# The folded scans of an attention and Fourier kernel: 64 rows of each half of the array instead of 48

## The chip, the cores and the metric

The kernel runs on one core of a Trainium2 chip. The metric is the device time of one execution in microseconds (us), here the median of three runs; lower is better.

## The reference, cut to what matters

Inputs: `x` of 2048 rows and 512 columns, `wqkv` (512 x 1536), `wo` (512 x 512), four Fourier matrices and a gate vector.

```
g = sigmoid((x * gate_w).sum(-1))
q, k, v = x @ wqkv, cut into 32 heads of 16 columns
p = softmax(q k^T / 4)              # each head: 2048 x 2048
a = (p v) @ wo
b = dft_seq_re @ (x @ dft_hid_re.T) - dft_seq_im @ (x @ dft_hid_im.T)
out = g * a + (1 - g) * b
```

All is float32. The softmax needs a shift for every row that lies near the row's largest score; the kernel gets it from a pass of its own over the scores, the *scan*. The scan's result only sets this shift, which cancels in the quotient.

## The kernel before, in words

**Two halves of the array.** Nearly every product on TensorE takes 64 of its 128 rows or fewer. `halves_of` (L199 to L203) issues two products, one in rows 0 to 63 and one in rows 64 to 127, which run side by side. Such a pair is called a *step* below. A float32 operand is split into an upper part (hi) and the rest (lo), and a product is the sum of hi*hi, hi*lo and lo*hi, three steps.

**Stages.** The first stage projects `x` to q, k and v (`project_t`, `project_s`) and applies the Fourier matrix of the columns; the second applies the Fourier matrix of the rows (the loop over `coef`, L711 to L777, whose products are `xy<-b,c` in the profile). Then comes the attention: 16 pairs of heads, in which the scores (L228), the exponential (L252, L260) and the product with the values (L806) alternate.

**Scans.** A pair of heads has 64 scans: 16 blocks of 128 queries by 4 chunks of 512 keys. A scan makes one product for each of the two heads: head j in rows 64j and up, with 128 queries standing and 512 keys moving. `row_loads` (L104 to L115) fills the two tiles `qs` and `ks` for one pair of heads by eight DMAs: for each half, 32 rows hold hi of a key's 16 numbers twice over against hi and lo of the query's, and 16 rows more hold lo of the key against hi of the query. So a product takes 48 of the 64 rows of its half.

**Scans beside the other products.** Scans are put between the steps of the first two stages by `beside` (L326): one scan every so many steps, set by `scan_at` (BESIDE 2.72, SWAP 2.97, PART 2.15). The first 64 scans (pair 0) are plain: one DVE reduction takes the maximum of both heads (L155). The next 644 are *folded* (`scan_folded`, L159): for a pair of key chunks a and b, DRAM holds a - b and b (`kf_d`). The product with a - b goes through ACT's Relu into a tile `fold` (L176); the product with b goes to DVE, which adds `fold` and takes the maximum (L178). So of two scans in turn, one gives ACT two operations and the next gives DVE two. A scan's second head is issued one scan late, so a step L172 on PE holds head 0 of scan n and head 1 of scan n - 1. The PSUM banks of folded scans are `d0`, `d1`, `k0`, `k1` (and for some stretches a spare pair), taken in turn by `bed` (L290): a bank is written again two scans after it was last written, and PE waits there until ACT or DVE has read it.

**Loads of the folded scans.** `load_scan_beside` (L320) calls `row_loads` for pair 0 with plain keys and for the 11 other pairs of this phase with `kf_d`, and issues the eight DMAs on SP's queue seven steps apart, between the loads of the Fourier coefficients (`craw`, L395) and the stores (L316). `ROWS` says at which scan; a folded pair's loads begin some 24 to 60 scans ahead of its first scan.

The scans after the 708th (L153, beside the attention) are plain and have 48 rows; the scores of the attention (L228) have 50.

Of the kernel before, what the change touches and what calls it, by code (L numbers as in the profile page):

```python
# [18 lines left out]
P = 128  # L19
S = 2048  # L20
D = 512
H = 32
DH = 16
# [43 lines left out]
def build(tc, xT, wqkv, wo, wrT, wiT, cr, ci, ct, gate, out):  # L67
    nc = tc.nc
    with ExitStack() as ctx:
# [7 lines left out]
        q_d = [dram.tile([P, 2, S], F32, name=f"q_d{f}") for f in range(ND)]  # L77
        k_d = [dram.tile([P, 2, S], F32, name=f"k_d{f}") for f in range(ND)]
        ks_d = [dram.tile([P, S], F32, name=f"ks_d{f}") for f in range(ND)]
        kf_d = [dram.tile([P, 2, S], F32, name=f"kf_d{f}") for f in range(ND)]  # L80
# [20 lines left out]

        scanned, used, unfolded = {}, {}, {}

        def row_loads(p, queue, keys=k_d):  # L104

            qs = stk.tile([P, S], F32R, tag="stk", name="qs")
            ks = stk.tile([P, S], F32R, tag="stk", name="ks")
            loads = []
            for j in range(2):
                b, r = 64 * j, slice(DH * ((2 * p + j) % 8), DH * ((2 * p + j) % 8) + DH)  # L110
                loads += [(ks[b:b + 32, :], keys[p // 4][r, 0:1, :].to_broadcast([DH, 2, S])),
                          (qs[b:b + 32, :], q_d[p // 4][r, :, :].rearrange("e n s -> (e n) s")),
                          (ks[b + 32:b + 48, :], keys[p // 4][r, 1, :]),
                          (qs[b + 32:b + 48, :], q_d[p // 4][r, 0, :])]
            return (qs, ks), [lambda dst=dst, src=src: queue.dma_start(dst.bitcast(F32), src) for dst, src in loads]  # L115

        def load_scan(p):
            if p < NP:
                scanned[p], loads = row_loads(p, nc.sync)
                for load in loads:  # L120
                    load()

        def load_use(p, spread=False):
            if p < NP:
                used[p], loads = row_loads(p, nc.sync)
                for load in loads:
                    load()
                    if spread:
                        yield
                qs, ks = used[p]  # L130
                for j in range(2):
                    b = 64 * j + 48
                    nc.sync.dma_start(ks[b:b + 2, :].bitcast(F32), ones_d)
                    for n in range(2):
                        nc.sync.dma_start(qs[b + n:b + n + 1, :].bitcast(F32),
                                          m_d[p][n:n + 1, :, j].rearrange("n g b k -> n b g k"))
# [3 lines left out]
        def new_maxima(p):  # L140
            mx[p] = (sm.tile([P, 2, NB, 4], F32, tag="mx_end", name="mx", bufs=1) if p == END_PAIR else
                     sm.tile([P, 2, NB, 4], F32, tag="mx", name="mx"))
# [16 lines left out]
        def scan_folded(n, j, bank, pool):  # L159

            p, i = SEQ[n]
            qb, c = i // 4, i % 4
            if i == 0 and j == 0:
                new_maxima(p)
                if p in PARTS:
                    nc.vector.memset(mx[p], -3.0e38)
            qs, ks = scanned[p]  # L170
            b, ps = 64 * j, bank(n, j)
            nc.tensor.matmul(ps, qs[b:b + 48, qb * P:(qb + 1) * P], ks[b:b + 48, c * 512:(c + 1) * 512],  # L172
                             start=True, stop=True)
            if c % 2 == 0:
                fold[j] = pool.tile([P, 512], F32, tag=f"fold{j}", name="fold")
                nc.scalar.activation(fold[j], ps, AF.Relu)  # L176
            else:
                nc.vector.tensor_tensor_reduce(out=fold[j], in0=ps, in1=fold[j], scale=1.0, scalar=-3.0e38,  # L178
                                               op0=ALU.add, op1=ALU.max, accum_out=mx[p][:, j, qb, c // 2:c // 2 + 1])
# [56 lines left out]
        def bank():  # L236

            order_.append(order_.pop(0))
            return narrow(order_[-1], "s2")
# [29 lines left out]
        with ExitStack() as pf:  # L269
# [31 lines left out]
            def after(n, f, *args):  # L301

                count[0] += 1
                due.append((slots[0] + n, count[0], f, args))
# [11 lines left out]
                    d[2](*d[3])  # L316

            def load_scan_beside(p):
                scanned[p], loads = row_loads(p, nc.sync, kf_d if p else k_d)
                for n, load in enumerate(loads):  # L320
                    after(7 * n, load)

# [3 lines left out]
            def beside():  # L326

                slots[0] += 1
                run_due()
                if pace[0] is None:  # L330
                    return
                pace[1] += 1.0 / pace[0]
                while seen[0] < FRONT and pace[1] >= 1.0:
                    pace[1] -= 1.0
                    n = seen[0]
                    if n == FOLDED.start:
                        begin_folds()
                    if n in ROWS:
                        load_scan_beside(ROWS[n])
                    if n not in FOLDED:  # L340
                        scan(n, s1())
                        done = n
                    else:

                        scan_folded(n, 0, *beds)
                        done = behind(n - 1)
                    seen[0] += 1
                    if seen[0] == FRONT:
                        done = behind(n)
                    if done is not None and SEQ[done][1] == SCANS - 1:  # L350
                        for d, part in enumerate(shift(SEQ[done][0], nc.scalar.copy, nc.gpsimd.tensor_sub)):
                            maxima.append(part)
                            after((3, 8, 26, 31, 36)[d], part)
# [3 lines left out]
            def behind(n):  # L357
                if n in FOLDED:
                    scan_folded(n, 1, *beds)
                    return n  # L360
# [59 lines left out]
            with ExitStack() as px:  # L420
# [185 lines left out]
                for n, (w, dst, f, c) in enumerate(order):  # L606
                    lead = s1() if n in (0, 2, 4, 6) else None
                    project_t(w, dst, f, c, lead and (lead[:, 0, :], lead[:, 1, :]))
                    if n == 7:
                        gate_sums()  # L610
                after(22, load_scan_beside, 0)
                after(84, scan_at, PACE)
                for f, c in [(2, 0), (3, 0)] + [(f, c) for f in range(1, ND) for c in range(1, NC)]:
# [60 lines left out]
            with ExitStack() as py:  # L674
# [36 lines left out]
                for n, (ph, t, u) in enumerate(coef):  # L711
# [38 lines left out]
                    for w in range(CS):  # L750
                        s = u * CS + w
# [29 lines left out]
        with ExitStack() as pa:  # L781
# [443 lines left out]
            for step in range(NP * PERIODS):  # L1225
                p, i = step // PERIODS, step % PERIODS
# [133 lines left out]
```

## Time and profile before

| | |
|---|---|
| median of 3 runs | 1714.61 us (1714.26 to 1715.05) |
| the profiled execution | 1714.2 us, span 1712.4 us from first to last instruction |
| PE busy | 1701.0 us, 99% of the span |
| ACT, DVE, POOL busy | 1492.3, 1188.9, 765.4 us |
| chain that ended last | 97% PE |
| stretch of the folded scans | 133.7 to 653 us |
| granted TensorE clock | 0.999 of full speed |

The profile is of one execution. Its chain of work that ended last is followed back from the last instruction; 97% of it is TensorE. A line of a group gives the program line, engine, operation, the tile written and the tiles read, partitions x elements, the count, the busy time and the mean of one. PE stands for the products, PEld for the loads of the standing operand, which overlap them. Products run side by side and are pipelined, so their mean duration is longer than the time from one to the next.

### The profile page before, as it was taken

Reading aid. Unit: us, or ns where it says so; the run is one execution under the profiler, and the core shown is the slowest. Engines: PE = TensorE matmul, PEld = TensorE weight load, DVE = VectorE, ACT = ScalarE, POOL = GpSimd, SP = SyncE. Lnnn points to the kernel's source line nnn. Section 1 sums busy time; section 2 is a strip of 40 time slices with the busy share of each in tenths; the row PEclk is TensorE's granted clock in tenths of the full one; section 3 lists DMA queues with packets and bytes.
Section 4 is the critical chain, followed back from the end, with each engine's and each line's share of the span. In section 5 each row is a group of like instructions: output and inputs, shape, how many; then the busy total and the mean of one; then the engine's idle time right before and its main releaser. Section 6 shows DMA issues by size and latency. Waiting matters only on the chain.

```text
span 1712.4 us, 36306 instructions
## 1 busy us (share of the span) xinstructions
PE 1701.0 (99%) x13560; PEld 1022.5 (60%) x13560; DVE 1188.9 (69%) x2179; ACT 1492.3 (87%) x2472; POOL 765.4 (45%) x909
## 2 busy tenths in 40 slices
PE   9999999999999999999999999999999999999998
PEld 6888888989988885333333333333345555555554
DVE  5898888889899996666666666666742556654343
ACT  6447889888888888999999999999998888889876
POOL 3672435755555762433535455353423333334222
PEclk9999999999999999999999999999999999999999
DMA  7783457533337665356544445353436465566733
GB/s 255 244 288 77 149 161 217 160 111 108 105 105 206 175 133 101 94 132 141 137 112 113 121 117 132 100 130 79 98 71 145 133 150 148 141 171 156 195 90 127
DMA packets 148961, 240.96 MB, mean 141 GB/s; under 512 B 50048, under 2 KB 60784, under 8 KB 142192
## 3 DMA queue, kind: packets, MB, share of 16 engines
q1 hardware_dynamic: 133520, 217.27, 47.1%
q0 software_dynamic: 14688, 20.33, 5.1%
q8 instruction: 106, 1.74, 0.5%
q10 hardware_dynamic: 576, 1.05, 0.2%
q14 instruction: 71, 0.58, 0.1%
HBM read 158.34 MB, written 81.01 MB: 140 GB/s over the span
## 4 chain that ended last, share of the span: by engine, by line
PE 97%; DMA 1%; DVE 0%; issue 0%; ACT 0%; SPq 0%; DVEq 0%; ACTq 0%
PE pvb L806 29%; PE xy L203 26%; PE s L228 19%; PE s L172 9%; PE s L203 8%; PE s L153 5%; DMA q_d<-eh 0%; DMA raws<-wqkv 0%; DMA raws<-xT 0%; PE s L595 0%; DVE y L921 0%; DVE fold L178 0%; ACT fold L176 0%; SPq L565 0%; SPq L564 0%
## 5 line engine op out<-in xcount | busy, mean ns | idle before, releaser
L252 ACT ACTIVATE eb<-s 128x1024 f32<-128x1024 f32 x512 | 581.0, 1135 | 59.8 <-PE s L228 59.7
L260 ACT ACTIVATE e<-s 128x512 f32<-128x512 f32 x1022 | 611.0, 713 | 0.0
L155 DVE TENSOR_REDUCE mx<-s 128x2 f32<-128x1024 f32 x380 | 460.9, 1224 | 196.5 <-PE s L153 196.3
L806 PE MATMUL pvb<-eb,va 128*17 128x512 f32 x2052 | 514.5, 597 | 0.0
L806 PE MATMUL pvb<-e,va 128*17 128x512 f32 x2044 | 513.6, 597 | 0.0
L178 DVE CUSTOM_DVE_ANT_0 fold<-s,fold 128x512 f32<-128x512 f32 x644 | 433.2, 690 | 57.0 <-PE s L172 30.4
L176 ACT ACTIVATE fold<-s 128x512 f32<-128x512 f32 x644 | 377.4, 602 | 81.3 <-PE s L172 61.8
L228 PEld LDWEIGHTS s<-qs,ks 50*128 50x128 f32 x2048 | 214.3, 184 | 361.6 <-ACT eb L252 269.2
L228 PE MATMUL s<-qs,ks 50*128 50x512 f32 x2048 | 424.3, 435 | 0.0
L203 PE MATMUL xy<-b,c 64*128 64x512 f32 x2448 | 390.9, 393 | 0.3 <-ACT c L371 0.3
L172 PE MATMUL s<-ks,qs 48*128 48x512 f32 x1288 | 315.4, 402 | 1.5 <-DVE mx L178 0.9
L203 PEld LDWEIGHTS xy<-b,c 64*128 64x128 f32 x2448 | 284.0, 187 | 30.5 <-issue 1.0
L172 PEld LDWEIGHTS s<-ks,qs 48*128 48x128 f32 x1288 | 171.3, 184 | 36.1 <-DVE mx L178 9.9
L806 PEld LDWEIGHTS pvb<-eb,va 128*17 128x17 f32 x2052 | 69.8, 96 | 189.1 <-issue 179.5
L153 PE MATMUL s<-ks,qs 48*128 48x512 f32 x760 | 153.2, 394 | 0.0
L203 PE MATMUL s<-b,b 64*128 64x512 f32 x1050 | 136.8, 391 | 0.0
L825 POOL DMA_DIRECT2D r_d<-lc x31 | 18.0, 580 | 262.2 <-DVE lc L824 213.7
L203 PE MATMUL xy<-w,b 64*128 64x512 f32 x768 | 114.8, 392 | 0.0
L203 PEld LDWEIGHTS s<-b,b 64*128 64x128 f32 x1050 | 100.2, 185 | 23.7 <-issue 1.0
L818 POOL DMA_DIRECT2D lc<-ob x124 | 63.0, 515 | 114.6 <-DVE ob L815 109.3
L403 POOL TENSOR_TENSOR c<-craw,c 128x512 fp32r<-128x512 f32 x84 | 110.2, 1312 | 6.7
L827 POOL DMA_DIRECT2D rb<-r_d x124 | 60.5, 495 | 107.0 <-DMA r_d<-lc 101.8
(149 smaller groups left out, 1560.9 us busy)
## 6 DMA issues: line engine op xcount, KB each, us to landing
qs<-q_d SPq DMA_DIRECT2D x68, 256.0 KB
craw<-cr SPq DMA_DIRECT2D x60, 256.0 KB
craw<-ct SPq DMA_DIRECT2D x48, 256.0 KB
ks<-k_d SPq DMA_DIRECT2D x46, 256.0 KB
kept_None<-sum SPq DMA_DIRECT2D x40, 256.0 KB
craw<-kept_None SPq DMA_DIRECT2D x40, 256.0 KB
qs<-q_d SPq DMA_DIRECT2D x68, 128.0 KB
craw<-ci SPq DMA_DIRECT2D x32, 256.0 KB
```

The lines of the kernel that those rows point to most:

```text
L153: nc.tensor.matmul(ps[:, j, :], qs[b:b + 48, qb * P:(qb + 1) * P], ks[b:b + 48, c * 512:(c + 1) * 512], start=True, stop=True)
L155: nc.vector.tensor_reduce(mx[p][:, :, qb, c], ps, axis=AX.X, op=ALU.max)
L172: nc.tensor.matmul(ps, qs[b:b + 48, qb * P:(qb + 1) * P], ks[b:b + 48, c * 512:(c + 1) * 512], start=True, stop=True)
L176: nc.scalar.activation(fold[j], ps, AF.Relu)
L178: nc.vector.tensor_tensor_reduce(out=fold[j], in0=ps, in1=fold[j], scale=1.0, scalar=-3.0e38, op0=ALU.add, op1=ALU.max, accum_out=mx[p][:, ...
L203: nc.tensor.matmul(ps[j], lhs[r], rhs[r], start=first, stop=last)
L228: nc.tensor.matmul(pss[j], ks[b:b + 50, kb * P:(kb + 1) * P], qs[b:b + 50, q0:q0 + 512], start=True, stop=True)
L252: nc.scalar.activation(e, ps, AF.Exp, scale=SCALE)
L260: nc.scalar.activation(e[j], pss[j], AF.Exp, scale=SCALE)
L403: sub(lo, raw, hi.bitcast(F32))
L806: nc.tensor.matmul(pvb[r:r + VC, :], va[:, kb, 2 * p + j, :], es[c][j], start=kb == 0, stop=kb == NB - 1, tile_position=(0, r))
L818: nc.gpsimd.dma_start(lc[32 * n:32 * n + 32, :], ob[r + DH:r + VC, :].rearrange("p (s e) -> p s e", e=16))
```

## The change

`row_loads` gets an argument `square`, which `load_scan_beside` sets for every pair but pair 0. With it, the last two loads of each half have 32 rows instead of 16: lo of the key twice over against hi and lo of the query. So 16 rows more carry lo*lo. The products of `scan_folded` read 64 rows instead of 48. Pair 0's scans, the scans beside the attention and the scores keep their rows.

```
-        def row_loads(p, queue, keys=k_d):
+        def row_loads(p, queue, keys=k_d, square=False):
...
-                          (ks[b + 32:b + 48, :], keys[p // 4][r, 1, :]),
-                          (qs[b + 32:b + 48, :], q_d[p // 4][r, 0, :])]
+                          *([(ks[b + 32:b + 64, :], keys[p // 4][r, 1:2, :].to_broadcast([DH, 2, S])),
+                             (qs[b + 32:b + 64, :], q_d[p // 4][r, :, :].rearrange("e n s -> (e n) s"))] if square else
+                            [(ks[b + 32:b + 48, :], keys[p // 4][r, 1, :]),
+                             (qs[b + 32:b + 48, :], q_d[p // 4][r, 0, :])])]
...
-            nc.tensor.matmul(ps, qs[b:b + 48, qb * P:(qb + 1) * P], ks[b:b + 48, c * 512:(c + 1) * 512],
+            nc.tensor.matmul(ps, qs[b:b + 64, qb * P:(qb + 1) * P], ks[b:b + 64, c * 512:(c + 1) * 512],
...
-                scanned[p], loads = row_loads(p, nc.sync, kf_d if p else k_d)
+                scanned[p], loads = row_loads(p, nc.sync, kf_d if p else k_d, p > 0)
```

No instruction changes its place on any engine. On SP's queue, at the loads of the second folded pair in the first stage, before the change (lines of `row_loads`: L115; `ab_d` is a store of the other work; the last numbers are the rows and the row's elements):

```order
L115 DMA ks<-kf_d_87 32x1x2048
L115 DMA qs<-q_d_75 32x2048
L316 DMA ab_d_118<-ab 128x512
L115 DMA ks<-kf_d_87 16x2048
L115 DMA qs<-q_d_75 16x2048
```

and with it (lines are two further on):

```order
L117 DMA ks<-kf_d_87 32x1x2048
L117 DMA qs<-q_d_75 32x2048
L318 DMA ab_d_118<-ab 128x512
L117 DMA ks<-kf_d_87 32x1x2048
L117 DMA qs<-q_d_75 32x2048
```

The order stays; the second load of each tile is twice as large. On PE, in the second stage, two folded scans among the steps of the Fourier products (a row with x2 is a step; its shape is that of the result), before:

```order
L172 MATMUL s<-ks,qs 128x512 x2
L203 MATMUL xy<-b_4856,c 128x512 x2
L203 MATMUL xy<-b_4855,c 128x512 x2
L172 MATMUL s<-ks,qs 128x512 x2
L203 MATMUL xy<-b_4886,c 128x512 x2
```

and with the change:

```order
L174 MATMUL s<-ks,qs 128x512 x2
L205 MATMUL xy<-b_4856,c 128x512 x2
L205 MATMUL xy<-b_4855,c 128x512 x2
L174 MATMUL s<-ks,qs 128x512 x2
L205 MATMUL xy<-b_4886,c 128x512 x2
```

The rows are the same but for their line numbers: only the number of array rows that L172 reads differs, which a row of this list doesn't show.

## The prediction

> **What bounds the kernel now.** I read the page first (busy shares and the chain that ended last), then a table of stretches for PE, then the timeline of PE at three places, then the waits. The page says that TensorE is the bound nearly everywhere:
>
> ```profile
> PE 1701.0 (99%) x13560; PEld 1022.5 (60%) x13560; DVE 1188.9 (69%) x2179; ACT 1492.3 (87%) x2472; POOL 765.4 (45%) x909
> PE 97%; DMA 1%; DVE 0%; issue 0%; ACT 0%; SPq 0%; DVEq 0%; ACTq 0%
> ```
>
> The change touches products of L172 alone, so the question is what a step (two products side by side, one in each half) costs there. The mean durations of the groups say nothing about rows: 48 rows take 402 ns, 64 rows take 393 ns, and their weight loads 184 and 187 ns.
>
> ```profile
> L172 PE MATMUL s<-ks,qs 48*128 48x512 f32 x1288 | 315.4, 402 | 1.5 <-DVE mx L178 0.9 <-ACT fold L176 0.6
> L203 PE MATMUL xy<-b,c 64*128 64x512 f32 x2448 | 390.9, 393 | 0.3 <-ACT c L371 0.3
> L172 PEld LDWEIGHTS s<-ks,qs 48*128 48x128 f32 x1288 | 171.3, 184 | 36.1 <-DVE mx L178 9.9 <-ACT fold L176 6.0
> L203 PEld LDWEIGHTS xy<-b,c 64*128 64x128 f32 x2448 | 284.0, 187 | 30.5 <-issue 1.0
> ```
>
> But products overlap, so a duration is not what a step costs; the distance from one step to the next is. The table of stretches gives it (stretch: its length, PE busy, number of products touched, clock, DMA share, GB/s):
>
> ```profile
> 40.00:57.00 17.00, 17.00 (x152) 1.00 0.84 268
> 60.00:131.00 71.00, 71.00 (x612) 1.00 0.73 253
> 133.70:304.10 170.40, 169.99 (x1435) 1.00 0.55 156
> 304.10:650.30 346.20, 345.08 (x2894) 1.00 0.51 137
> ```
>
> The count takes in the product that already runs on each half when the stretch begins, so steps are (count - 2) / 2. In 40 to 57 us, where only 64-row products run, a step costs 17.00 / 75 = 0.2267 us. In 60 to 131 us, where plain scans of 48 rows stand among them, 71.00 / 305 = 0.2328. In the two stretches of folded scans, 170.40 / 716.5 = 0.2378 and 346.20 / 1446 = 0.2394. The clock is full in all four. So something in the stretches with scans costs about 5% of every step, and PE counts as busy while it pays.
>
> **Where the excess sits.** The timeline of PE around plain scans, 80 to 84 us (start, length, what, count), has nothing waiting:
>
> ```profile
> 80.10 0.40 PE L153 MATMUL s<-ks,qs 48*128 48x512 f32 x2
> 80.34 1.32 PE L203 MATMUL xy<-b,c 64*128 64x512 f32 x10
> 81.50 0.40 PE L153 MATMUL s<-ks,qs 48*128 48x512 f32 x2
> 81.73 1.32 PE L203 MATMUL xy<-b,c 64*128 64x512 f32 x10
> 82.89 0.40 PE L153 MATMUL s<-ks,qs 48*128 48x512 f32 x2
> ```
>
> From scan to scan there are six steps in 1.395 us (80.10 to 82.89, halved). Six pure steps are 6 x 0.2267 = 1.360. So each scan of 48 rows brings about 0.035 us that no pure step has. Over the whole stretch: 71.00 - 305 x 0.2267 = 1.9 us, and L153 has 120 products there, 60 scans, so **0.031 us a scan**:
>
> ```profile
> L153 PE MATMUL s<-ks,qs 48*128 48x512 f32 x120 | 24.0, 396 | 0.0
> ```
>
> Is it the 48 rows, or only the change of tensors and banks that comes with any scan? The end of the program has 64-row products that go on in another PSUM bank after every third step and switch between operands:
>
> ```profile
> 1702.29 0.62 PE L203 MATMUL s<-b,chi 64*128 64x512 f32 x4
> 1702.74 0.40 PE L203 MATMUL s<-b,clo 64*128 64x512 f32 x2
> ...
> 1703.65 0.62 PE L203 MATMUL s<-b,chi 64*128 64x512 f32 x4
> 1704.10 0.40 PE L203 MATMUL s<-b,clo 64*128 64x512 f32 x2
> 1704.33 0.39 PE L203 MATMUL pvb<-b,chi 64*128 64x512 f32 x1
> ```
>
> From 1702.29 to 1704.33 there are nine steps (x4, x2, three times over): 2.04 / 9 = 0.2267. Changing banks and operands costs nothing as long as all have 64 rows. What is left to set a scan apart is its 48 rows and that its operands lie in the tiles `qs` and `ks`. I take the rows to be the cause; the trace has no 64-row product from those tiles, so this is a conclusion by elimination.
>
> Against it stands a row of the same kind after a break of another sort: after four transposes the six steps from 36.30 take 1.49 us, 0.13 more than 1.360. Part of that is the first product's own filling, but it shows that a disturbed stream of 64-row products may take some steps to settle, whatever disturbed it.
>
> ```profile
> 35.71 0.66 PE L316 MATMUL s<-ident,zr 128*128 128x128 f32 x4
> 36.30 1.66 PE L203 MATMUL xy<-b,c 64*128 64x512 f32 x12
> 37.79 1.53 PE L203 MATMUL xy<-b,w 64*128 64x512 f32 x12
> ```
>
> The Trainium skill speaks against the change here. Its page "TensorE: Matmul & The Clock Gate", section "LDWEIGHTS (loading the stationary operand)", has the time of a weight load follow from the columns and not from the contracted rows, and its section "Why this matters for your kernels" gives a single product of 32 rows the time of one of 128. The mean durations above (184 and 187, 402 and 393 ns) agree with that; the distances between steps are not what it speaks of. By that rule the change leaves PE as it is and the time is the one before; it is the second rival below.
>
> **The change part by part.**
>
> *Products.* 1288 products (644 steps) get 64 rows; count and order on PE stay. The excess of the two folded stretches over pure steps is 170.40 - 716.5 x 0.2267 = 8.0 and 346.20 - 1446 x 0.2267 = 18.4, together 26.4 us. Not all of it comes from rows; some is PE waiting for a bank:
>
> ```profile
> PEld s L172 <- DVE mx L178: 9.4, 36, 0.9
> PEld s L172 <- ACT fold L176: 6.0, 16, 0.8
> PE s L172 <- DVE mx L178: 0.9, 3, 0.4
> PE s L172 <- ACT fold L176: 0.6, 2, 0.4
> ```
>
> These are 16.9 us of waits (133.7 to 650.3 us) in 52 weight loads and 5 products. A wait holds one half while the other goes on, and both halves wait much alike, so in time of PE I count half: 8.4 us. What is left, 26.4 - 8.4 = **18.0 us**, is the most that the rows can give back. It agrees with 644 steps x 0.031 = 20.0 from the plain scans.
>
> *What the faster PE meets.* The scan's place in the program is fixed, so ACT and DVE get their work sooner. In the second stretch DVE is the fuller:
>
> ```profile
> 304.10:650.30 346.20, 345.08 (x2894) 299.61 (x2892) 313.65 (x925) 286.68 (x515) 205.38 (x208) 1.00 0.51 137
> ```
>
> DVE is busy 313.65 of 346.20 us (third pair of numbers after the length; ACT is the fourth), so it has 9.4% to spare. With PE quicker by the 18.0 us times this stretch's share of the excess (18.4 / 26.4), it is 12.5 us shorter, and DVE has 6.0% to spare. If waits go as the inverse of what is to spare, they rise by 9.4 / 6.0 = 1.57, from 8.4 to 13.2 us: **4.8 us are given back**. The bounds are nothing (the waits stay) and all that the second stretch wins, 12.5 us. And after each wait the stream must settle again; some 52 x 1.57 = 82 waits at the 0.031 us of a scan's disturbance keep **2.5 us** of the excess (bounds 0 and 5).
>
> *Loads.* 22 loads of `ks`, and as many of `qs` with them, grow from 128 to 256 KB:
>
> ```profile
> ks<-kf_d SPq DMA_DIRECT2D x22, 128.0 KB
> ```
>
> That is 44 x 0.131 = 5.8 MB more in the two stretches, which move 156 GB/s x 170.4 us + 137 GB/s x 346.2 us = 74 MB at a DMA share of 0.51 to 0.55. That is 8% more for queues that are half idle, and no wait above names a DMA. The tightest is the first folded pair: its last load is issued at 121.97 and its first product runs at 133.7 us,
>
> ```profile
> 121.97 0.43 SPq L115 DMA_DIRECT2D qs<-q_d  x1
> L172 PE MATMUL s<-ks,qs x1288: 386/397/500, 133.7 to 653.0; 48*128 48x512 f32 x184
> ```
>
> 11.7 us apart, and 0.5 MB more at the 253 GB/s of that stretch are 2 us. So I cost the loads at nothing; their cover is that distance, and without it they cost the 2 us there. DMA issues keep their number, so SP's queue is not longer.
>
> *Sum.* 18.0 - 4.8 - 2.5 = 10.7 us less. What follows the folded scans is bound by PE too and keeps its instructions, so the gain is carried to the end. 1714.2 (the profiled execution; its span is 1712.4) - 10.7 = 1703.5; the median of the runs is 0.4 above the profiled one, which gives 1703.9. With all of the 18.0 it would be 1696.6; with the waits doubled (8.4 given back) and 5 us of settling, 1710.0.
>
> **The rivals.**
>
> *Bank waits eat the second stretch.* There PE turns from one bank to its next use in two scans, two steps of L172 and 2 x 2.15 others, 6.3 x 0.2394 = 1.51 us, which would shrink to 1.43, while the product, ACT's or DVE's operation (602 and 690 ns) and their queueing don't shrink.
>
> ```profile
> L178 DVE CUSTOM_DVE_ANT_0 fold<-s,fold 128x512 f32<-128x512 f32 x644 | 433.2, 690 | 57.0 <-PE s L172 30.4 <-ACT fold L176 10.9 <-PE xy L203 0.9
> L176 ACT ACTIVATE fold<-s 128x512 f32<-128x512 f32 x644 | 377.4, 602 | 81.3 <-PE s L172 61.8 <-DVE mx L178 3.2
> ```
>
> For it: 36 of the 52 waits of weight loads are for DVE, which is 91% busy. Against it: 1.43 is still over twice DVE's 0.69, and a spare of 6% is left. Then only the first stretch gains. Its own waits, 133.7 to 304.1 us, are 4.9 us:
>
> ```profile
> PEld s L172 <- DVE mx L178: 2.7, 12, 0.3
> PEld s L172 <- ACT fold L176: 1.8, 4, 0.8
> PE s L172 <- ACT fold L176: 0.4, 1, 0.4
> ```
>
> 8.0 less half of them is 5.5, less 1 for settling 4.5: 1714.6 - 4.5 = 1710.1.
>
> *Nothing changes on PE.* The excess comes with any scan (operands in `qs` and `ks`, or a single product between others), as the settling after the transposes suggests. Then 64 rows cost what 48 did and the time is 1714.6. Against it are the nine steps at the end of the program.
>
> *The larger loads come late: slower.* Between 545 and 602 us both last pairs are loaded, 1.05 MB more, beside the reload of the other operand:
>
> ```profile
> 545.30:602.40 57.10, 56.23 (x465) 1.00 0.66 181
> ```
>
> At its 181 GB/s that is 5.8 us of transfers. If PE gains nothing and those loads of coefficients that stand behind them on SP's queue land just when they are needed, PE stops for as long: 1714.6 + 5.8 = 1720.4. It decides from the point where the queue's spare, now 34% of 57.1 or 19 us, lies elsewhere than where the loads are. Nothing in the waits of PE shows a DMA there now.
>
> **How the numbers follow.** Chances: forecast 0.68 (own range 1697 to 1710), bank waits 0.08 (1710), nothing 0.18 (1714.6), slower 0.06 (1720). About 0.2%, 3.4 us, is what a measurement of this kernel can tell from no change. Faster by more than that (below 1711.2) are the forecast and half of the bank case: 0.72. Within: nothing, and the other half of the bank case: 0.22. Slower: 0.06. For 8 in 10 the forecast and the bank case, 0.76, are not enough, so the range goes on to the time of the second rival and takes a part of its runs: 1699 to 1715.
>
> **What would show it.** Right: in the profile of the changed kernel the two folded stretches are together 8 to 14 us shorter with the same counts; a step there comes down from 0.2378 and 0.2394 us to some 0.233 to 0.235; the stretches 40 to 57 and 60 to 131 us don't change; the waits of L174's weight loads for DVE and ACT rise from 15.4 us; the attention takes as long as before. Wrong: the folded stretches keep 0.238 and 0.239 a step with the same waits (rows are not the cause), or the steps get shorter and the waits take all of it, or a DMA stands among PE's waits.

## The result and the profile after

The changed kernel takes **1711.41 us** (median of 15 runs, 1710.38 to 1714.72) against 1714.61 before (15 runs, 1713.74 to 1715.52): ratio 0.9981, 95% interval 0.9974 to 0.9989. It is 3.2 us faster; 10.7 were forecast. The profiled execution took 1711.22 us. PE is the bound as before:

```profile
span 1709.4 us, 36306 instructions
PE 1697.7 (99%) x13560; PEld 1022.3 (60%) x13560; DVE 1187.3 (69%) x2179; ACT 1491.7 (87%) x2472; POOL 764.3 (45%) x909
PE 97%; DMA 1%; DVE 0%; issue 0%; ACT 0%; SPq 0%; DVEq 0%; ACTq 0%
```

The table of stretches for PE (length, PE busy, products touched, clock, DMA share, GB/s), cut at the same products as before; lines of the code are two further on:

```profile
40.00:57.00 17.00, 17.00 (x154) 1.00 0.85 269
60.00:131.00 71.00, 71.00 (x610) 1.00 0.74 260
134.00:303.95 169.95, 169.55 (x1435) 1.00 0.57 166
303.95:647.60 343.65, 342.41 (x2891) 1.00 0.54 149
```

The first folded stretch is 0.45 us shorter, the second 2.55: together 3.0 of the 3.2 us. A step of the folded stretches now costs 169.95 / 716.5 = 0.2372 and 343.65 / 1444.5 = 0.2379 us (0.2378 and 0.2394 before); it was forecast at 0.233 to 0.235, and a pure step is 0.2267. The waits for PSUM banks hardly rose, from 16.9 to 18.2 us (133.7 to 650.3 us; us in total, times, longest):

```profile
PEld s L174 <- DVE mx L180: 10.4, 39, 0.9
PEld s L174 <- ACT fold L178: 6.3, 17, 0.8
PE s L174 <- DVE mx L180: 0.9, 3, 0.5
PE s L174 <- ACT fold L178: 0.6, 2, 0.4
```

So the gain was not eaten by waits: it didn't come up. The timeline of PE in the second stretch shows it, where nothing waits. Before:

```profile
340.53 0.56 PE L172 MATMUL s<-ks,qs 48*128 48x512 f32 x2
340.77 0.79 PE L203 MATMUL xy<-b,c 64*128 64x512 f32 x4
341.24 0.55 PE L172 MATMUL s<-ks,qs 48*128 48x512 f32 x2
341.47 0.80 PE L203 MATMUL xy<-b,c 64*128 64x512 f32 x4
341.94 0.56 PE L172 MATMUL s<-ks,qs 48*128 48x512 f32 x2
342.18 1.01 PE L203 MATMUL xy<-b,c 64*128 64x512 f32 x6
342.87 0.55 PE L172 MATMUL s<-ks,qs 48*128 48x512 f32 x2
```

With the change:

```profile
340.07 0.59 PE L174 MATMUL s<-ks,qs 64*128 64x512 f32 x2
340.30 0.82 PE L205 MATMUL xy<-b,c 64*128 64x512 f32 x4
340.76 0.59 PE L174 MATMUL s<-ks,qs 64*128 64x512 f32 x2
341.00 0.81 PE L205 MATMUL xy<-b,c 64*128 64x512 f32 x4
341.46 0.59 PE L174 MATMUL s<-ks,qs 64*128 64x512 f32 x2
341.69 1.05 PE L205 MATMUL xy<-b,c 64*128 64x512 f32 x6
342.38 0.39 PE L174 MATMUL s<-ks,qs 64*128 64x512 f32 x1
```

Ten steps (x2, x4, x2, x4, x2, x6) take 2.34 us before and 2.31 with the change, 0.234 and 0.231 a step, and pure ones would take 2.27. Something of a scan's disturbance went with the rows, and more than half of it stayed.

### The profile page after: what moved, and what is told of

Read it like the earlier page. It is cut to its first block, busy times and chain, and to the rows that moved or that the text cites. A ratio compares the mean times of both kernels' runs of the same rounds, so it can differ in the third digit from the quotient of the medians.

```text
span 1709.4 us, 36306 instructions
## 1 busy us (share of the span) xinstructions
PE 1697.7 (99%) x13560; PEld 1022.3 (60%) x13560; DVE 1187.3 (69%) x2179; ACT 1491.7 (87%) x2472; POOL 764.3 (45%) x909
## 4 chain that ended last, share of the span: by engine, by line
PE 97%; DMA 1%; DVE 0%; issue 0%; ACT 0%; SPq 0%; DVEq 0%; ACTq 0%
PE pvb L808 29%; PE xy L205 26%; PE s L230 19%; PE s L174 9%; PE s L205 9%; PE s L155 5%; DMA q_d<-eh 0%; DMA raws<-wqkv 0%; DMA raws<-xT 0%; PE s L597 0%; DVE y L923 0%; DVE fold L180 0%; ACT fold L178 0%; SPq L567 0%; SPq L566 0%
## 5 line engine op out<-in xcount | busy, mean ns | idle before, releaser
L808 PE MATMUL pvb<-e,va 128*17 128x512 f32 x2044 | 513.6, 597 | 0.0
L174 PE MATMUL s<-ks,qs 64*128 64x512 f32 x1288 | 319.2, 401 | 1.6 <-DVE mx L180 0.9
L174 PEld LDWEIGHTS s<-ks,qs 64*128 64x128 f32 x1288 | 173.9, 184 | 36.3 <-DVE mx L180 10.8
L155 PE MATMUL s<-ks,qs 48*128 48x512 f32 x760 | 153.4, 394 | 0.0
```

The costliest lines, as they stand in the source:

```text
L155: nc.tensor.matmul(ps[:, j, :], qs[b:b + 48, qb * P:(qb + 1) * P], ks[b:b + 48, c * 512:(c + 1) * 512], start=True, stop=True)
L174: nc.tensor.matmul(ps, qs[b:b + 64, qb * P:(qb + 1) * P], ks[b:b + 64, c * 512:(c + 1) * 512], start=True, stop=True)
L808: nc.tensor.matmul(pvb[r:r + VC, :], va[:, kb, 2 * p + j, :], es[c][j], start=kb == 0, stop=kb == NB - 1, tile_position=(0, r))
```

## The experiments

The theory on record was **rows**: a scan disturbs the stream of PE because it takes 48 rows among products of 64. The rivals formed after the result: the larger loads ate a larger gain; the rest of the disturbance comes with the **operands**, the tiles `qs` and `ks` themselves; or with the **place in the program**, a single product in another bank between others.

### The larger loads alone

```
-            nc.tensor.matmul(ps, qs[b:b + 64, ...], ks[b:b + 64, ...],
+            nc.tensor.matmul(ps, qs[b:b + 48, ...], ks[b:b + 48, ...],
```

> The larger loads of the change, but products of 48 rows as before. If the larger loads cost nothing, as the prediction had it, the time is that of before, 1714.6 us, and the folded stretches have 0.2378 and 0.2394 us a step. If the gain of the rows was larger and the loads ate it, this run is slower than before by the part that is missing, up to 7 us (1721).

Measured: 1714.67 us against 1714.83 of before on that chip, ratio 1.0001 (0.9991 to 1.0010). The loads cost nothing beyond that interval, some 1.7 us at most; they did not eat a gain of 7. (Its profiled execution, at 1715.36 us, has folded stretches 1.2 us longer than before, which is within the spread of its runs, 1714.29 to 1716.92.)

### 56 rows

> The change with 56 rows in each folded product instead of 64 (eight of the rows with the lower parts of the keys are left out of the maxima). If what a scan costs goes with the number of rows that are missing, the time lies half way between before and the change, 1713.0 us, and the step behind a scan, 241 ns for 48 rows and some 234 for 64, takes about 237. If only the full 64 helps, it is 1714.6; if any number over 48 does, 1711.4.

Measured: 1714.72, ratio 0.9998 (0.9989 to 1.0007). Its folded stretches are as long as before:

```profile
134.20:304.40 170.20, 169.79 (x1436) 1.00 0.57 165
304.40:650.60 346.20, 345.07 (x2892) 1.00 0.55 148
```

Eight more rows bring nothing, sixteen bring 3.2 us. It doesn't go with the number of missing rows: of 48, 56 and 64, only the full 64 is another case (all with the tiles where the change has them).

### Plain scans with 64 rows

```
+                e = b + (64 if n < SCANS else 48)
-                nc.tensor.matmul(ps[:, j, :], qs[b:b + 48, ...], ks[b:b + 48, ...], ...)
+                nc.tensor.matmul(ps[:, j, :], qs[b:e, ...], ks[b:e, ...], ...)
```

> The change, and the 64 plain scans of the first pair with 64 rows too (they stand among steps of 64 rows with nothing waiting, four to six steps apart). Theory rows: the rows are all of a scan's disturbance where nothing waits, so the stretch of 60 to 131 us goes from 0.2328 to 0.2267 us a step, 1.9 us shorter, 1709.5 in all. Theory rest: a scan of 64 rows still disturbs the stream, as the first folded scan in the trace of the change seems to (steps of 235, 234, 232 ns behind it instead of 233, 242, 233), so only a quarter to a third of 0.031 us a scan goes: 0.5 us, 1710.9.

Measured: 1712.20, ratio 0.9984 (0.9975 to 0.9994), no gain over the change. By theory rows it had to be 1709.5. The time alone doesn't settle it, because DVE is nearly full in that stretch and the time can't follow a faster PE there (see the last run below). The timeline does. Here the two halves issue a scan's products one after the other (79.74 and 79.99):

```profile
79.74 0.39 PE L156 MATMUL s<-ks,qs 64*128 64x512 f32 x1
79.76 0.60 PE L206 MATMUL xy<-b,c 64*128 64x512 f32 x2
79.99 0.39 PE L156 MATMUL s<-ks,qs 64*128 64x512 f32 x1
80.20 1.11 PE L206 MATMUL xy<-b,c 64*128 64x512 f32 x8
...
83.90 0.39 PE L156 MATMUL s<-ks,qs 64*128 64x512 f32 x1
```

From 79.74 to 83.90 there are three scans in 18 steps: 4.16 us, 0.2311 a step, where theory rows has 0.2267 and 48 rows gave 0.2325 (1.395 / 6). With nothing waiting and 64 rows everywhere, most of the extra is still there, so **rows alone fall as the whole cause**. What went is a quarter at most, as theory rest has it.

### The operands of the other products

```
         def halves_of(ps, lhs, rhs, first, final):
+            recent[:] = lhs, rhs
...
-            nc.tensor.matmul(ps, qs[b:b + 64, ...], ks[b:b + 64, ...],
-                             start=True, stop=True)
+            nc.tensor.matmul(ps, recent[0][b:b + 64], recent[1][b:b + 64], start=True, stop=True)
```

> The change, but each folded scan's product repeats the operands of the last product of the other work (so the maxima and the softmax's shift are of other numbers, and the exponentials are taken of scores scaled to almost nothing); its bank, its place, its waits on ACT and DVE and its 64 rows stay, and the tiles qs and ks are loaded but not read. Theory operands: what is left of a scan's disturbance comes with the tiles qs and ks; then steps go to some 0.229 to 0.231 us in the folded stretches (they have 0.2365 and 0.2369 in the change), and the time falls by another 8 to 12 us, to about 1701. Theory place: it comes with a single product in another bank between others, or with the waits; then the time stays at 1711.

Measured: 1706.70, ratio 0.9954 (0.9939 to 0.9969): 4.7 us under the change, with as many products of the same shape at the same place, in the same banks, with the same engines to wait for. So the rest of the disturbance comes with what is read, and theory place in the program falls. The further gain is 4.7 us, not the 8 to 12 that were expected, and a step of the folded stretches comes to 0.235 us, not 0.229 to 0.231 (in the change it was 0.2372 and 0.2379, as above, not the 0.2365 and 0.2369 of that text). One reason is that the waits for banks rose, from 18.2 to 22.1 us.

### Where the operands lie

What can make `qs` and `ks` differ from other operands of the same shape? The addresses that the build gives: in every partition, `b`, `c` and `w` begin 1632 bytes beyond a multiple of 2048 (or a multiple of 512 from that, for weights), `qs` and `ks` at 960 beyond one. The distance is 672 bytes: the pool `sm` between them takes 2720 bytes, 672 more than 2048, and every other tile between them takes a multiple of 2048. Two kinds are said to lie alike modulo some number if their distance is a multiple of it. The runs that follow only shift tiles: a tile of some bytes that nobody reads, in the pool `sm` behind `qs` and `ks` (moves all others), or in `keep` ahead of them (moves both). Shown with 8 columns, 32 bytes; the later runs have 24, 56 and 88 columns, 96, 224 and 352 bytes.

```
+        pad = sm.tile([P, 8], F32, name="pad", bufs=1)
+        nc.vector.memset(pad, 0.0)
+        pad0 = keep.tile([P, 8], F32, name="pad0")
+        nc.vector.memset(pad0, 0.0)
```

The first guess was the offset from a multiple of 64 bytes, in which they differ by 32.

> The change, and a tile of 32 bytes that nobody reads ahead of the other operands in SBUF. In all kernels so far qs and ks begin at multiples of 64 bytes in a partition and the operands of all other products 32 bytes beyond one; with it all begin at multiples of 64. Theory alignment: what is left of a scan's disturbance at 64 rows is the turn from operands at one offset to operands at the other; then folded steps come near 0.2267 us, as they did with the other work's operands, and the time is some 4.5 us under the change, 1706.7; if the offset of 32 itself also costs something in pure steps, the whole kernel gains more. Theory tile: it is something else of qs and ks (that DMAs write them, where they lie); then it stays at 1711.4.

> The change with the 32 bytes ahead of qs and ks too, so both kinds move by 32: qs and ks begin 32 beyond a multiple of 64 and all others at multiples. Theory alignment: the turn between offsets stays, 1711.4, and pure steps show whether 32 or 0 is better in itself (0.2267 us a step in 40 to 57 us if it makes no difference). Theory tile: 1711.4.

> The change with 32 bytes at both places: all operands begin 32 beyond a multiple of 64. Theory alignment, if only likeness counts: 1706.7 as with all at multiples of 64. If multiples of 64 count in themselves, it is the slower of the two. Theory tile: 1711.4.

Measured: 1711.21 (0.9971 to 0.9990 of before), 1710.80 (0.9967 to 0.9986) and 1711.16 (0.9972 to 0.9991). All three are where the change is. Likeness modulo 64 is not it, and shifting both kinds together (the second) does nothing.

> The kernel before (48 rows) with the same 32 bytes. Under theory alignment the offsets and the rows are two disturbances. If they add, it is 4.5 us under before, 1710.1, and behind the run with 64 rows by the 3.2 us of the change. If the disturbance is one and comes once for either cause, it stays at 1714.6, since 48 rows are enough to bring it. Under theory tile it stays at 1714.6 too; the run before this one tells these apart.

Measured: 1710.67, ratio 0.9977 (0.9968 to 0.9987). Neither answer that was written for a failure of the alignment theory (1714.6) came: with 704 bytes between the two kinds, **48 rows are as good as 64** (1711.21 with 64). So the place of the operands counts, if not modulo 64, and what the rows are worth depends on it. That called for a shift in which the two kinds lie alike altogether. Laying the pool of small tiles ahead of `qs` and `ks` does that, at no cost in bytes and with every other tile at its old address:

```
-        stk = ctx.enter_context(tc.tile_pool(name="stk", bufs=6))
         sm = ctx.enter_context(tc.tile_pool(name="sm", bufs=2))
+        stk = ctx.enter_context(tc.tile_pool(name="stk", bufs=6))
```

> The change with the pool of small tiles (2720 bytes) laid ahead of qs and ks instead of behind them, so qs and ks begin 2720 bytes later and everything else stays. The operands of the other products all begin at 1632 beyond a multiple of 2048 bytes (or some 512 further, for weights); qs and ks began at 960 and now begin at 1632. Theory place in the partition: a scan disturbs the stream because its operands lie at another offset, modulo 512 or 2048, than the others'; then it behaves as with the other work's own operands and the time is about 1706.7 us, some 4.5 under the change, with steps of 0.227 to 0.229 where nothing waits. Theory repeat: the run with the other work's operands was quicker because it read the same operands again; then this one stays at 1711, as the shifts by 32 bytes did.

> The kernel before (48 rows) with the pools laid that way. If the place in the partition is all that counts and the rows only shift how the two places meet, 48 rows do as well as 64: 1706.7. If rows are a cause of their own, it lies behind the run with 64 rows by 2 to 4 us: 1709 to 1711. Theory repeat: 1714.6, or 1711 as with the 32 bytes.

Measured: with 64 rows **1705.90**, ratio 0.9949 (0.9937 to 0.9962); with 48 rows 1712.31, ratio 0.9988 (0.9979 to 0.9997). Theory repeat falls and theory place in the partition holds, but only with 64 rows: 6.4 us lie between the two. Place alone brought 2.3 us, rows alone 3.2, both together 8.7. The folded stretches, with 64 rows in place:

```profile
134.40:302.40 168.00, 167.52 (x1435) 1.00 0.57 167
302.40:642.30 339.90, 338.49 (x2893) 1.00 0.56 149
```

and with 48 rows in place:

```profile
133.50:303.30 169.80, 169.37 (x1435) 1.00 0.55 156
303.30:648.30 345.00, 343.80 (x2893) 1.00 0.51 138
```

507.9 us against 514.8, and 513.6 in the change, 516.6 before. With 64 rows in place, a step of the second stretch is 339.90 / 1445.5 = 0.2351. The timeline shows why it isn't 0.2267:

```profile
360.76 0.58 PE L174 MATMUL s<-ks,qs 64*128 64x512 f32 x2
360.99 0.80 PE L205 MATMUL xy<-b,c 64*128 64x512 f32 x4
361.45 0.57 PE L174 MATMUL s<-ks,qs 64*128 64x512 f32 x2
361.68 0.80 PE L205 MATMUL xy<-b,c 64*128 64x512 f32 x4
362.13 0.57 PE L174 MATMUL s<-ks,qs 64*128 64x512 f32 x2
362.39 0.76 PE L205 MATMUL xy<-b,c 64*128 64x512 f32 x4
363.09 0.50 PE L174 MATMUL s<-ks,qs 64*128 64x512 f32 x2
```

Six steps from 360.76 take 1.37 us, 0.228 each; the next three take 0.96, because the product at 363.09 waited for its bank (its weight load stood 0.36 us until ACT had read it). More than half of what is left in these stretches is waits, as worked out below.

From the last product of the folded scans to the end of the program, the change and all runs that shift tiles take 1058.9 to 1059.6 us, and the kernel before 1059.4: what the shifts bring lies in the folded stretches.

The rows leave a mark in the weight loads of the *other* products, the place doesn't. In 304 to 640 us, before:

```profile
L203 PEld LDWEIGHTS xy<-b,c 64*128 64x128 f32 x1938 | 233.8, 187 | 20.0
```

in place with 48 rows:

```profile
L203 PEld LDWEIGHTS xy<-b,c 64*128 64x128 f32 x1946 | 232.8, 187 | 20.5
```

and in the change, not in place, with 64:

```profile
L205 PEld LDWEIGHTS xy<-b,c 64*128 64x128 f32 x1952 | 234.2, 184 | 18.8
```

187 ns with 48-row scans among them, 184 with 64. The scans' own weight loads take 184 ns in all three. This mark isn't the cost itself: with 704 bytes between the kinds it is there too (187 ns with 48 rows, 184 with 64), though the times there are alike.

### Which distance counts

> The change with 96 bytes behind qs and ks, so that the two kinds lie 768 bytes apart modulo 2048 (672 in the change): alike modulo 256, not modulo 512. Theory place, if 256 bytes or fewer are what counts: 1706.7; if 512 or more: 1710 to 1712. Theory repeat: 1710 to 1712.

> The change with 352 bytes there, 1024 apart modulo 2048: alike modulo 1024 and 512, not modulo 2048. Theory place, if up to 1024 bytes are what counts: 1706.7; if 2048: 1710 to 1712. Theory repeat: 1710 to 1712.

> The change with 224 bytes behind qs and ks: 896 bytes apart modulo 2048, alike modulo 128, not modulo 256. If 128 bytes or fewer count, 1705.4 as with 768; if it takes 256, some 1711 as with 704 (alike modulo 64).

Measured, with the others, all with 64 rows:

| bytes apart, modulo 2048 | alike modulo | us | ratio to before (95%) |
|---|---|---|---|
| 672 (the change) | 32 | 1711.41 | 0.9974 to 0.9989 |
| 704 | 64 | 1711.21 | 0.9971 to 0.9990 |
| 896 | 128 | 1709.37 | 0.9956 to 0.9980 |
| 768 | 256 | 1705.36 | 0.9932 to 0.9959 |
| 1024 | 1024 | 1704.88 | 0.9932 to 0.9960 |
| 0 | 2048 | 1705.90 | 0.9937 to 0.9962 |

256 bytes are enough, 64 bring nothing, and 128 lies between (its interval touches those above it). The three last don't differ by more than their intervals; they are the best versions found, about 9 us or 0.5% under the kernel before. That the change's 64 rows are needed was tried for the last alone (1712.31 with 48).

### Is that all of a scan's disturbance?

> qs and ks at the others' place (small tiles ahead of them), folded scans of 64 rows, and the 64 plain scans of the first pair with 64 rows too. If rows and place are all of a scan's disturbance, nothing is left of it where nothing waits: the stretch of 60 to 131 us has 0.2267 to 0.227 us a step (0.2328 before) and the time is 1.5 to 1.9 us under the run with 48 rows in the plain scans, 1704.2. If a scan has a third cost of its own, the stretch stays at 0.230 or more and the time falls by less than 1 us.

Measured: 1705.74, ratio 0.9945 (0.9931 to 0.9958), no gain over 1705.90, and a step of the stretch costs 71.00 / 308.5 = 0.2301 us. By these two numbers it is the answer that was written for a third cost. But the timeline shows otherwise where nothing waits:

```profile
80.66 0.50 PE L156 MATMUL s<-ks,qs 64*128 64x512 f32 x2
80.88 1.41 PE L206 MATMUL xy<-b,c 64*128 64x512 f32 x10
82.02 0.50 PE L156 MATMUL s<-ks,qs 64*128 64x512 f32 x2
82.24 1.41 PE L206 MATMUL xy<-b,c 64*128 64x512 f32 x10
83.38 0.50 PE L156 MATMUL s<-ks,qs 64*128 64x512 f32 x2
```

Twelve steps with two scans take 2.72 us, 0.2267 each: a scan with 64 rows whose operands lie alike costs no more than any other step, where it cost 0.035 us extra before. **Where nothing waits, rows and place are all of it.** The time did not follow because DVE, which takes the plain scans' maxima, is full there (length, PE, PEld, DVE busy of 60 to 131 us in this run):

```profile
60.00:131.00 71.00, 71.00 (x619) 65.18 (x617) 70.73 (x65) 32.87 (x61) 51.92 (x41) 1.00 0.74 260
```

and the one group of waits of PE's weight loads in 60 to 134 us (us, count, longest), which had 0.5 us in 2 waits before:

```profile
PEld s L156 <- DVE mx L158: 1.4, 5, 0.4
```

DVE is busy 70.73 of 71.00 us (70.46 before, so it had next to nothing to spare); PE gets through 308.5 steps instead of 305 and then waits for DVE's banks. That expectation missed by taking the stretch for bound by PE alone.

## Why the prediction was wrong, point by point

- *A pure step costs 0.2267 us, a scan brings 0.031 to 0.035 more while PE counts as busy.* Right, and shown by taking it away in the last run, where no wait stands between.
- *"I take the rows to be the cause", by elimination.* **This is the step that failed.** The sentence ahead of it names both things that set a scan apart, "its 48 rows and that its operands lie in the tiles `qs` and `ks`", and the argument went on with one. The nine steps at the end of the program were taken as proof that operands don't matter; but those operands lie a multiple of 512 bytes apart (the tiles between them take multiples of 2048), so they could not test it. The term of 18.0 us for the rows needed rows and place together. Rows alone gave 3.0 us in the folded stretches; 56 rows gave none.
- *Waits give back 4.8.* In the change they rose by half of 18.2 - 16.9, 0.7 us, since PE gained little. In the run in place with 64 rows, where the stretches are 8.7 us shorter, the waits of 133.7 to 650.3 us are 21.2 us:

```profile
PEld s L174 <- DVE mx L180: 13.0, 47, 0.9
PEld s L174 <- ACT fold L178: 6.4, 17, 0.9
PE s L174 <- DVE mx L180: 1.1, 3, 0.5
PE s L174 <- ACT fold L178: 0.7, 2, 0.4
```

  Half of 21.2 - 16.9 is 2.2 us. The rule of the spare share, with the stretch at 339.90 us and DVE's 313.65, gives 8.4 x 9.4 / 7.7 - 8.4 = 1.9: about right.
- *Settling keeps 2.5.* Too small, as far as it can be told: in place the folded stretches exceed pure steps by 507.9 - 2162 x 0.2267 = 17.8 us, and 17.8 less half of the waits, 10.6, leaves 7.2. That this is settling after some 70 waits is inferred, not measured by itself.
- *The sum.* With rows and place, the mechanism as priced would have given 10.7 and gave 8.7 (1705.90). The change as it stood met one of the two conditions and gave 3.2.
- *Loads cost nothing.* Right within 1.7 us: the run with the loads alone, and no DMA among PE's waits.
- *The gain is carried to the end.* Right: 3.0 us in the folded stretches, 3.2 in all.
- *The rivals.* Bank waits and late loads did not come. "Nothing changes on PE" was given 0.18 and named the operands in `qs` and `ks` as one of two reasons; it was true of most of the excess, not of all. By the rule of the Trainium skill quoted there (the page "TensorE: Matmul & The Clock Gate", section "LDWEIGHTS (loading the stationary operand)") the contracted rows don't set the time of a weight load; the trace agrees for a scan's own, 184 ns with 48 and with 64 rows. The prediction carried this rule over to the whole of PE for that rival, and the stream around the scans did change with the rows.

The range, 1699 to 1715, held the time, because it was stretched to the time of the rival without a gain; the gain was 3.2 us, under a third of the 10.7.

## What to carry to other kernels

Where PE counts as fully busy, divide a stretch by its steps and compare it with the purest stretch of the program: most of a loss of 5% stood here in no wait, and no mean duration gave its size. If products of one kind disturb the stream, look at two things before the schedule: whether they fill their half of the array like the others, and where their operands lie; here reordering two pools was worth 5.5 us on top of the change's 64 rows, and 2.3 without them. And when an elimination leaves two candidates, price both, and both together.

## What the runs showed of the hardware that was not expected

- A product of 48 or 56 rows among products of 64 disturbs the steps around it: 1714.6 us with 48 and 1714.7 with 56 at 672 bytes, against 1711.4 with 64; in place 1712.3 with 48, against 1705.9 with 64.
- 64-row products whose operands lie alike modulo 256, 1024 or 2048 bytes follow each other at 0.227 us (the median distance in 310 to 540 us in each of the three runs); at 672 bytes apart it is 0.232, at 704 0.233. At 704 apart, rows make no difference (1710.67 with 48, 1711.21 with 64), at 672 they are worth 3.2 us, in place 6.4: the two causes don't add.
- Why it is 256 bytes, and why rows and place act together, the traces don't show; the length of neighbouring weight loads (187 and 184 ns) goes with the rows, and with neither the place nor the time. This stays open.
